# Two more head groups' queries and keys by seven block products, maxima 22 steps ahead, five partial head products early

## The chip, the cores and the metric

One core of a Trainium2 chip runs the kernel as one program. The time is the device time of the program on that core, in microseconds (us). Its engines work side by side, each through its own instructions in order: PE (TensorE) multiplies matrices into PSUM banks of 128 x 512 floats, ACT (ScalarE) and DVE (VectorE) read PSUM and SBUF, POOL (GpSimd) works on SBUF, and SP (SyncE) here issues all DMAs.

## The reference

Multi-head attention (32 heads of 16) and a gated feed-forward layer on the same input, mixed by a sigmoid of `x . gate_w`; all in float32, with S = 2048 tokens, D = 512, F = 1792.

```python
qkv = (x @ wqkv).reshape(B, S, 3, H, Dh).transpose(2, 0, 3, 1, 4)
p = softmax(einsum("bhqd,bhkd->bhqk", q, k) * Dh ** -0.5)
a = einsum("bhqk,bhkd->bhqd", p, v).transpose(0, 2, 1, 3).reshape(B, S, D) @ wo
b = (sigmoid(x @ w_gate) * (x @ w_up)) @ w_down
g = sigmoid((x * gate_w).sum(-1, keepdims=True))
return g * a + (1 - g) * b
```

## The kernel before

A float32 operand is split into a high part and a rest (`xh`, `xl`), and a product is three matmuls on the parts (`terms`). The program has four stages.

**Front and values.** Queries and keys of head group 0 (of four groups of eight heads) are computed (line 612), stored to DRAM (`q_d`, `k_d`) and loaded back for head pair 0 (`load_pair`, line 238). Then come the values of all heads (the loop at line 655), 192 slots of two half-height matmuls each. Between the slots, `first_max` issues the first score products for the row maxima: each call is two matmuls (line 284) and two DVE reductions (line 286). They start at slot 20.

**Steps.** The loop `for k in range(NPER)` has 256 steps; a head pair takes 16 of them. A step has eight score products for the exponentials (line 648, then ACT's `Exp`, line 650), the product of exponentials and values (line 781, 16 matmuls by the profile), eight score products for the maxima of a later pair (lines 284 and 286), and twelve half-height matmuls of "fill" (line 161). The maxima run LEAD = 20 half-steps ahead, so that they end at step FREE = 246. The last ten steps (order `LAST`) have no maxima and six fill matmuls. Row maxima of half a pair go through POOL (`put_max`) to DRAM and back as extra rows of the queries (line 308). `load_pair` of the next pair stands at a pair's first step.

**Fill** is a generator, `filling`, that hands out one product at a time: queries and keys of head groups 1 to 3 (`"qk"`, 24 matmuls a product), gate and up projections (`"far"`, `"side"`, `"chain"`) and the first half of the output product of EARLY = 3 blocks of 256 queries (`"heads"`). Gate and up are done with seven block products in place of eight (the weights' quarters and x's quarters are added and subtracted first, and the results added afterwards on POOL, lines 507 to 517). Weights are split on POOL. POOL's work is put into a list, `later` (additions, weights and splits in order of arrival), and `work(length)` issues some of it at two places of a step; `slow` holds the mixing of x. The two halves of a fill product write one PSUM bank: between the halves `turn` puts an empty instruction into POOL's order that waits for the first half, and the second half waits for it.

**Tail.** The hidden layer times `w_down` (line 966, 28 chunks of 24 matmuls), and for eight blocks u of 256 queries the product with `wo` (`heads_out`, line 940): 24 matmuls, or 12 where `u < EARLY`, which then add the first half from DRAM (`hp_d`).

PE, ACT, DVE and POOL run in the written order. The order of SP's DMAs is set by the scheduler that builds the program.

## Time and profile before

| | |
|---|---|
| median of 3 runs (lowest to highest) | 1694.38 us (1693.39 to 1695.08) |
| the profiled execution's own time | 1694.23 us |
| its span, first to last instruction | 1692.5 us |
| DMA over the span | 223.51 MB, mean 132 GB/s |
| granted clock of PE | 1.000 |

Rows of the profile name an engine, a line of the kernel, an operation, the tile written and the tiles read. A busy time counts overlapping instructions once; the mean of one instruction is its latency and can be longer than the distance to the next. In brackets stands the idle time before an instruction and what ended it.

### The profile page before, as it was taken

To read this page: it belongs to the slowest core of one execution; us is meant where nothing else is said; L and a number is where in the kernel's file an instruction comes from. 1 tells how busy PE (TensorE), PEld (TensorE's weight loads), DVE (VectorE), ACT (ScalarE), POOL (GpSimd) and SP (SyncE) were. 2 spreads that over 40 slices of the span, in tenths; PEclk is the share of its full clock that TensorE was granted. 3 is DMA by queue.
4 is the path that set the end of the run, shared out by engine and by line. 5 is a ranking of instruction groups with operands and counts; after the bars stand their busy time and mean duration, and the time that the engine had idled before them with its cause. 6 is when DMAs were issued, how large, how long until landed. Compare 5 with 4: busy or idle time off the path is not lost.

```text
span 1692.5 us, 34518 instructions
## 1 busy us (share of the span) xinstructions
PE 1685.8 (100%) x12509; PEld 1032.5 (61%) x12509; DVE 1446.7 (85%) x2333; ACT 1357.4 (80%) x2643; POOL 880.7 (52%) x862
## 2 busy tenths in 40 slices
PE   9999999999999999999999999999999999999999
PEld 7755555555555555555555555555555555568887
DVE  6988888888889989999888888889988888887643
ACT  4188888888898989888888989889898988984321
POOL 1033343447664555554666667676666667643110
PEclk9999999999999999999999999999999999999999
DMA  7412324254755352534625353535353434478762
GB/s 235 109 45 65 83 64 96 64 127 153 200 171 136 109 120 92 118 114 106 193 98 136 108 144 108 139 108 135 108 126 108 127 120 132 142 234 280 266 195 71
DMA packets 126922, 223.51 MB, mean 132 GB/s; under 512 B 23520, under 2 KB 33504, under 8 KB 123872
## 3 DMA queue, kind: packets, MB, share of 16 engines
q1 hardware_dynamic: 126752, 221.31, 44.9%
q8 instruction: 98, 1.61, 0.4%
q14 instruction: 72, 0.59, 0.1%
HBM read 131.33 MB, written 89.92 MB: 131 GB/s over the span
## 4 chain that ended last, share of the span: by engine, by line
PE 96%; DMA 1%; DVE 1%; POOL 1%; issue 0%; SPq 0%; ACT 0%; POOLq 0%; DVEq 0%
PE dn L161 30%; PE sm L781 27%; PE sm L284 12%; PE st L648 7%; PE sm L966 5%; PE sm L648 5%; PE st L284 2%; PE dn L966 2%; PE st L161 2%; PE st L966 2%; PE st L148 1%; PE st L612 1%; PE sm L148 1%; DVE stat L286 1%; DMA gul<-gu_d 1%
## 5 line engine op out<-in xcount | busy, mean ns | idle before, releaser
L286 DVE TENSOR_REDUCE stat<-sm 128x1 f32<-128x512 f32 x1310 | 848.5, 683 | 150.8 <-PE sm L648 129.6
L650 ACT ACTIVATE p<-st 128x512 f32<-128x512 f32 x1020 | 617.7, 652 | 1.4 <-PE st L648 0.8
L650 ACT ACTIVATE p<-sm 128x512 f32<-128x512 f32 x1026 | 608.8, 630 | 0.9 <-PE sm L648 0.9
L284 PE MATMUL sm<-ks,qs 48*128 48x512 f32 x1310 | 516.4, 435 | 0.3 <-DVE stat L286 0.3
L286 DVE TENSOR_REDUCE stat<-st 128x1 f32<-128x512 f32 x738 | 482.1, 681 | 0.1
L781 PE MATMUL sm<-p,v 128*17 128x512 f32 x4032 | 482.1, 595 | 0.0
L648 PE MATMUL sm<-qs,ks 64*128 64x512 f32 x1026 | 426.9, 419 | 0.3 <-DMA qs<-max_d 0.3
L648 PE MATMUL st<-qs,ks 64*128 64x512 f32 x1020 | 426.9, 419 | 0.2 <-DVE stat L286 0.2
L284 PEld LDWEIGHTS sm<-ks,qs 48*128 48x128 f32 x1310 | 233.9, 184 | 290.9 <-DVE stat L286 208.6
L798 POOL TENSOR_TENSOR sum<-sum,part 128x512 f32<-128x512 f32 x224 | 288.9, 1290 | 181.2 <-PE sm L648 169.1
L284 PE MATMUL st<-ks,qs 48*128 48x512 f32 x738 | 291.3, 395 | 0.0
L786 ACT ACTIVATE part<-sm 128x512 f32<-128x512 f32 x215 | 128.7, 599 | 133.0 <-issue 106.8
L781 PEld LDWEIGHTS sm<-p,v 128*17 128x17 f32 x4032 | 93.6, 96 | 227.2 <-issue 156.7
L648 PEld LDWEIGHTS st<-qs,ks 64*128 64x128 f32 x1020 | 187.7, 184 | 30.2 <-issue 3.4
L648 PEld LDWEIGHTS sm<-qs,ks 64*128 64x128 f32 x1026 | 189.1, 185 | 9.5 <-issue 4.3
L514 POOL TENSOR_TENSOR chain<-chain,chain 128x512 f32<-128x512 f32 x84 | 108.5, 1291 | 114.6 <-PE sm L648 112.1
L514 POOL TENSOR_TENSOR had<-chain,had 128x512 f32<-128x512 f32 x84 | 108.1, 1287 | 59.6 <-PE sm L648 43.0
L284 PEld LDWEIGHTS st<-ks,qs 48*128 48x128 f32 x738 | 137.8, 187 | 1.0 <-ACT v L631 0.3
L514 POOL TENSOR_TENSOR side<-side,side 128x512 f32<-128x512 f32 x28 | 36.1, 1291 | 92.7 <-PE sm L648 87.1
L576 ACT ACTIVATE chain<-dn 128x512 f32<-128x512 f32 x112 | 77.8, 694 | 0.0
L103 POOL TENSOR_TENSOR ol<-ot,oh 128x1024 fp32r<-128x1024 f32 (+1 forms) x8 | 16.4, 2054 | 101.9 <-ACT oh L100 101.9
L311 POOL CAST mhl<-mt 128x32 fp32r<-128x32 f32 x32 | 7.4, 233 | 102.7 <-DVE mt L292 102.7
(837 smaller groups left out, 3205.3 us busy)
## 6 DMA issues: line engine op xcount, KB each, us to landing
gul<-gu_d SPq DMA_DIRECT2D x56, 512.0 KB
had<-gu_d SPq DMA_DIRECT2D x84, 256.0 KB
gu_d<-had SPq DMA_DIRECT2D x84, 256.0 KB
gu_d<-side SPq DMA_DIRECT2D x56, 256.0 KB
qs<-q_d SPq DMA_DIRECT2D x90, 128.0 KB
ks<-k_d SPq DMA_DIRECT2D x90, 128.0 KB
pv_d<-sum SPq DMA_DIRECT2D x32, 256.0 KB
gu_d<-far SPq DMA_DIRECT2D x28, 256.0 KB
```

The lines of the kernel that those rows point to most:

```text
L148: pe.matmul(o, a, b, start=(i == 0), stop=(i == len(ops) - 1))
L161: mm = pe.matmul(self.o, a[rows], b[rows], start=(self.n == 0), stop=(self.n == 2 * len(self.ops) - 1))
L284: pe.matmul(t, qs[r:r + KM, qt * P:(qt + 1) * P], ks[r:r + KM, g * 512:(g + 1) * 512], start=True, stop=True)
L286: dve.tensor_reduce(stat[half][:, b, qt % 8, g:g + 1], t, axis=AX.X, op=ALU.max)
L514: pool.tensor_tensor(to, u, w, ALU.add)
L576: leave = lambda e, o: act.activation(e, o, AF.Copy)
L648: pe.matmul(o, ks[r:r + KR, (kt + a) * P:(kt + a + 1) * P], qs[r:r + KR, q0:q0 + 512], start=True, stop=True)
L650: act.activation(pt[:, 2 * a + c, :], o, AF.Exp, scale=DH ** -0.5)
L781: pe.matmul(o[32 * c:32 * c + VW, :], v[:, 2 * k % 16 + a, h * VW:(h + 1) * VW], pts[c // 2][:, 2 * a + c % 2, :], start=(a == 0), stop=(a ...
L786: act.activation(e, o, AF.Copy)
L798: pool.tensor_tensor(s, s, e, ALU.add)
L966: pe.matmul(down[t], a, b, start=(f == 0 and m == 0), stop=(f == NF - 2 and m == 5))
```

## The change

Queries and keys of head groups 2 and 3 are no longer jobs `"qk"` of the fill: their weights go through `"far"`, `"side"` and `"chain"`, with seven block products in place of eight; the results gather in a new DRAM tensor `s_d`. `kept_x` saves the two parts of x that are overwritten for this and needed again. Sixteen new pieces, `split_load` and `split_sum`, load `s_d` back in steps 75 to 122, split it on POOL and store it to `q_d` and `k_d`. POOL's work on weights goes to a list of their own, `turnover`, behind the additions in `later`. LEAD is 22, so that FREE is 245 and `first_max` has 44 calls, from slot 10. EARLY is 5; for the two new blocks eight more reciprocals on DVE are done early (steps 202 to 211). `load_pair` has two loads a head and operand in place of three: one of 32 rows and one of 16, with rows interleaved.

```diff
--- before.py
+++ after.py
...
 KR = 64
-LEAD = 20
+LEAD = 22
...
 FREE = NPER - LEAD // 2
-EARLY = 3
+EARLY = 5
...
     rec_d = dram.tile([P, 512], F32, name="rec_d")
-    t_d = dram.tile([3, 2, 2, 2, P, 512], F32, name="t_d")
+    t_d = dram.tile([5, 2, 2, 2, P, 512], F32, name="t_d")
+    s_d = dram.tile([2, 2, P, S], F32, name="s_d")
...
         else:
-            split_later(h, l, raw)
+            split_later(h, l, raw, queue=turnover)
...
-    later, slow, soon = [], [], []
+    later, turnover, slow, soon = [], [], [], []
     def work(length):
-        while length > 0.3 and (later or slow):
-            cost, step = (later or slow).pop(0)
+        while length > 0.3 and (later or turnover or slow):
+            cost, step = (later or turnover or slow).pop(0)
...
         return [(w[k], (xh[:, k, cols], xl[:, k, cols])) for k in range(KT)]
-
-    FORM = {0: (0, 1, 0), 1: (0, 0, 1)}
...
             for b in range(2):
-                rows = slice((2 * p + b) * DH, (2 * p + b + 1) * DH)
-                for i, a in enumerate(FORM[t]):
-                    r = 64 * b + i * DH
-                    sp.dma_start((QS, KS)[t][p % 2][r:r + DH, cols].bitcast(F32), src[a, rows, cols])
+                rows, r = slice((2 * p + b) * DH, (2 * p + b + 1) * DH), 64 * b
+                to = (QS, KS)[t][p % 2]
+                if t == 0:
+                    two, one = src[:, rows, cols].rearrange("a d s -> d a s"), src[0, rows, cols]
+                else:
+                    two, one = src[0, rows, cols].unsqueeze(1), src[1, rows, cols]
+                    two = two.to_broadcast([DH, 2, cols.stop - cols.start])
+                sp.dma_start(to[r:r + 2 * DH, cols].bitcast(F32), two)
+                sp.dma_start(to[r + 2 * DH:r + KM, cols].bitcast(F32), one)
...
+    def kept_x(n, c, k0, cx):
+        cols = slice(cx * 512, (cx + 1) * 512)
+        for a, xs in enumerate((xh, xl)):
+            sp.dma_start(t_d[n, a, c].rearrange("k p s -> p k s"), xs[:, k0:k0 + 2, cols].bitcast(F32))
+
...
         pairs = [(m, i) for i in range(HF) for m in range(2)]
-        jobs = ([("qk", n) for n in range(1, D // P)] + [("far", i) for i in range(HF)]
-                + [("side", n) for n in pairs] + [("chain", n) for n in pairs] + [("heads", 0), ("down", 0)])
+        qk = [(2, 0), (3, 0)]
+        jobs = [("qk", 1)] + [("far", i) for i in range(HF + 1)]
+        for ns in (qk, pairs):
+            jobs += [("side", n) for n in ns] + [("chain", n) for n in ns]
+        jobs += [("heads", 0), ("down", 0)]
         gu_w = (w_gate, w_up)
+
+        def beside(m, i):
+            return i + HF if m < 2 else i + 1
...
                     raw = keep.tile([P, KT, P], F32, name=f"far{m}{n}r", tag="wr", bufs=2)
-                    sp.dma_start(raw[:, 2:], gu_w[m][n][:, 2:])
+                    sp.dma_start(raw[:, 2:], gu_w[m][n][:, 2:] if n < HF else wqk[2, 1, :, m])
...
             m, i = n
+            if m >= 2:
+                return [raw_weights(wqk[f, :, :, m - 2].rearrange("b p k f -> p b k f"), [P, KT, P],
+                                    f"{kind}{m}_{f}") for f in (2, 3)]
...
                 ks = slice(*ks)
-                split_later(h[:, ks], l[:, ks], src[:, ks], cost=0.33 * (ks.stop - ks.start))
+                split_later(h[:, ks], l[:, ks], src[:, ks], cost=0.33 * (ks.stop - ks.start), queue=turnover)
...
             def op(to, u, w, how):
-                later.append((0.65, lambda: pool.tensor_tensor(to, u, w, how)))
+                turnover.append((0.65, lambda: pool.tensor_tensor(to, u, w, how)))
...
         def place(m, f, c):
-            return gu_d[m, f, :, c * 512:(c + 1) * 512]
+            to = gu_d[m, f] if m < 2 else s_d[m - 2, f]
+            return to[:, c * 512:(c + 1) * 512]
...
                         yield run
-                        sp.dma_start(place(m, n, c), out_of(run, f"far{m}{n}_{c}"))
+                        sp.dma_start(place(m, n, c) if n < HF else place(2 + m, 0, c), out_of(run, f"far{m}{n}_{c}"))
...
                         yield run
-                        if n == pairs[-1]:
+                        if n in (qk[-1], pairs[-1]):
...
                             first = e
-                            sp.dma_start(place(m, i + HF, c + 2), e)
+                            sp.dma_start(place(m, beside(m, i), c + 2), e)
...
                 for c in range(2):
-                    to = [place(m, i, c), place(m, i, c + 2), place(m, i + HF, c + 2), place(m, i + HF, c)]
+                    i2 = beside(m, i)
+                    to = [place(m, i, c), place(m, i, c + 2), place(m, i2, c + 2), place(m, i2, c)]
...
                         yield run
+                        if n == qk[-1] and a >= 2:
+                            mixed_x(1 + a, c, 2 * a - 4, c + 2)
...
-            ks, q0 = slice(2 * (u // 2), 2 * (u // 2) + 2), (u % 2) * 256
+            ks, q0 = slice(u // 2 % 2 * 2, u // 2 % 2 * 2 + 2), (u % 2) * 256
...
-        ask = {"qk": (0, 3), "far": (0, 1), "side": (0, 1), "chain": (1, 3), "heads": (0, 1)}
+        ask = {"qk": (0, 3), "far": (0, 1), "side": (0, 1), "chain": (0, 1), "heads": (0, 1)}
...
                     if at == 4:
-                        for u in range(EARLY):
+                        for u in range(4):
...
                         first_heads_split(at - 6)
-                if kind == "heads" and at == 2:
-                    first_heads_split(2)
+                if kind == "heads" and at in (2, 4, 6):
+                    if at == 2:
+                        first_heads_load(4)
+                    first_heads_split(at // 2 + 1)
...
                     new = weights(*nxt, coming)
-                    end = later[-1]
+                    end = turnover[-1]
                 yield run
-            while end in later:
-                later.pop(0)[1]()
+            while end in turnover:
+                turnover.pop(0)[1]()
             ws = new
-            if kind == "far" and n == HF - 1:
+            if kind == "far" and n == HF:
...
                     mixed_x(0, c, 2, c)
+                for c in range(2):
+                    kept_x(3, c, 0, c + 2)
+                    kept_x(4, c, 2, c + 2)
...
             for m in range(3 * KT):
-                if 12 * (t + g) + m >= 20 + (192 - 20) * (2 * LEAD - len(first)) // (2 * LEAD):
+                if 12 * (t + g) + m >= 10 + (192 - 10) * (2 * LEAD - len(first)) // (2 * LEAD):
...
                 two[1].half(1 - g)
-                if (0, 0) in mrow and g == UP and m == 2:
+                if (0, 0) in mrow and m == 2:
...
+    split_in = {}
+
+    def split_load(r):
+        f, t, c = r // 8, r // 4 % 2, r % 4
+        e = split_in[r] = keep.tile([P, 2, 512], F32R, name=f"sq{r}", tag="ev", bufs=2)
+        sp.dma_start(e[:, 0, :].bitcast(F32), s_d[t, f, :, c * 512:(c + 1) * 512])
+
+    def split_sum(r):
+        f, t, c = r // 8, r // 4 % 2, r % 4
+        e = split_in.pop(r)
+
+        def store():
+            for a in range(2):
+                sp.dma_start((q_d, k_d)[t][a, (2 + f) * P:(3 + f) * P, c * 512:(c + 1) * 512],
+                             e[:, 1 - a, :].bitcast(F32))
+        split_later(e[:, 1, :], e[:, 0, :], e[:, 0, :].bitcast(F32), store)
+
...
-    dens = [denominators(0, 0, 32, 8), denominators(0, 32, 64, 2), denominators(1, 0, 64, 2)]
+    dens = [chain(denominators(0, 0, 32, 8), denominators(1, 0, 32, 8)), denominators(0, 32, 64, 2),
+            denominators(1, 32, 64, 2)]
...
             leave = dve.tensor_copy
-        if 78 <= k < 126:
-            t, r = divmod(k - 78, 6)
-            if r == 0:
+        if 75 <= k < 123:
+            t, r = divmod(k - 75, 6)
+            if r in (0, 3):
+                split_load(2 * t + r // 3)
+            if r in (1, 4):
+                split_sum(2 * t + r // 3)
+            if r == 1:
...
             exps = iter([early[0]] * 4 + [early[1]] * 4)
-        if 192 <= k < 202:
+        if 192 <= k < 212:
...
             next(dens[1])

```

In the tail of PE's order, here is block u = 3 of the output product, behind its chunk of the hidden layer (`wohl` is `wo`, `oh` and `ol` the heads' parts). Before:

```order
L966 MATMUL sm_70<-wd1h,hl_18595 128x512
L148 MATMUL sm_69<-wohl,oh_18598 128x512 x2
L148 MATMUL sm_69<-wohl,ol_18599 128x512
L148 MATMUL sm_69<-wohl,oh_18598 128x512 x2
L148 MATMUL sm_69<-wohl,ol_18599 128x512
L148 MATMUL sm_69<-wohl,oh_18598 128x512 x2
L148 MATMUL sm_69<-wohl,ol_18599 128x512
L148 MATMUL sm_69<-wohl,oh_18598 128x512 x2
L148 MATMUL sm_69<-wohl,ol_18599 128x512
L148 MATMUL st_65<-wohl,oh_18598 128x512 x2
```

and of the change:

```order
L1015 MATMUL sm_70<-wd1h,hl_18752 128x512
L149 MATMUL sm_69<-wohl,oh_18755 128x512 x2
L149 MATMUL sm_69<-wohl,ol_18756 128x512
L149 MATMUL sm_69<-wohl,oh_18755 128x512 x2
L149 MATMUL sm_69<-wohl,ol_18756 128x512
L149 MATMUL st_65<-wohl,oh_18755 128x512 x2
```

Each of the block's two products has 6 matmuls in place of 12, and the same holds for block u = 4: 24 matmuls fewer.

In POOL's order, here is a chain job (`had` and `chain` rows are additions of results, `sum` rows additions of attention sums, `mhl` rows the maxima, `ca`, `cb` and `chain_..r` rows the next job's weights). Before:

```order
L514 TENSOR_TENSOR chain_01_12679<-chain_01_12679,chain_00_12609 128x512
L514 TENSOR_TENSOR had_00_12546<-chain_01_12679,had_00_12546 128x512
L798 TENSOR_TENSOR sum_1_12366<-sum_1_12366,part_12699 128x512
L426 TENSOR_TENSOR chain_3r<-chain_3r,chain_10r 128x256
L426 TENSOR_TENSOR chain_10r<-chain_10r 128x256
L426 TENSOR_TENSOR chain_10r<-chain_10r,chain_3r 128x256
L138 CAST ca(0, 3)h<-chain_3r 128x512
L135 TENSOR_TENSOR ca(0, 3)l<-chain_3r,ca(0, 3)h 128x512
L138 CAST cb(0, 3)h<-chain_10r 128x512
L135 TENSOR_TENSOR cb(0, 3)l<-chain_10r,cb(0, 3)h 128x512
L514 TENSOR_TENSOR chain_02_12752<-chain_02_12752,chain_01_12679 128x512
```

and of the change:

```order
L842 TENSOR_TENSOR sum_1_12550<-sum_1_12550,part_13015 128x512
L444 TENSOR_TENSOR chain_3r<-chain_3r,chain_10r 128x256
L444 TENSOR_TENSOR chain_10r<-chain_10r 128x256
L444 TENSOR_TENSOR chain_10r<-chain_10r,chain_3r 128x256
L139 CAST ca(1, 3)h<-chain_3r 128x512
L536 TENSOR_TENSOR had_00_13000<-chain_00_13076,had_00_13000 128x512
L136 TENSOR_TENSOR ca(1, 3)l<-chain_3r,ca(1, 3)h 128x512
L139 CAST cb(1, 3)h<-chain_10r 128x512
L136 TENSOR_TENSOR cb(1, 3)l<-chain_10r,cb(1, 3)h 128x512
L536 TENSOR_TENSOR chain_01_13147<-chain_01_13147,chain_00_13076 128x512
```

The weights, seven instructions in one piece before, now stand where no addition is left to do, and an addition that comes up goes between them.

In SP's order, here are the loads of pair 1's queries and keys (`qs`, `ks`) and what stands behind them, in the values' stage. Before:

```order
L107 DMA qk_0r<-in_wqk_dram 128x512
L107 DMA qk_1r<-in_wqk_dram 128x512
L244 DMA qs_101<-q_d 16x2048 x6
L244 DMA ks_102<-k_d 16x2048 x6
L304 DMA max_d<-mhl_0_859 128x64
L308 DMA qs_99<-max_d 1x32x32 x4
```

and of the change:

```order
L247 DMA qs_102<-q_d 32x1x2048
L248 DMA qs_102<-q_d 16x2048
L247 DMA ks_103<-k_d 32x1x2048
L248 DMA ks_103<-k_d 16x2048
L366 DMA t_d<-xh 128x2x512
L366 DMA t_d<-xl 128x2x512
L308 DMA max_d<-mhl_0_831 128x64
L403 DMA far00r<-in_w_gate_dram 128x256
L312 DMA qs_100<-max_d 1x32x32 x4
```

Eight loads stand where twelve stood (four of them are shown), and four stores of x (`t_d`, two of them shown) now stand ahead of the first maxima.

## The prediction, made before the run

> **What bounds the kernel now.** I read the busy shares, then the stages, and then the steps one by one.
>
> ```profile
> PE 1685.8 (100%) x12509; PEld 1032.5 (61%) x12509; DVE 1446.7 (85%) x2333; ACT 1357.4 (80%) x2643; POOL 880.7 (52%) x862
> ```
>
> PE is never without work; a gain has to take matmuls off it, or pauses that its busy time hides. The view by stages (front, values, steps with maxima, steps without, tail; columns: length, then busy us of PE, weight loads, DVE, ACT, POOL) shows who could take over:
>
> ```profile
> 27.25:84.66 57.41, 56.72 (x469) 43.83 (x469) 50.29 (x83) 10.48 (x19) 4.16 (x6) 1.00 0.49 129
> 84.66:1461.20 1376.54, 1376.05 (x10827) 796.30 (x10826) 1227.36 (x2071) 1223.35 (x2446) 810.41 (x811) 1.00 0.42 119
> 1461.20:1498.04 36.84, 36.49 (x273) 16.38 (x269) 28.83 (x41) 36.35 (x76) 15.29 (x15) 1.00 0.33 111
> 1498.04:1692.50 194.46, 190.35 (x845) 155.54 (x844) 121.43 (x109) 70.06 (x76) 42.48 (x20) 1.00 0.65 213
> ```
>
> In the steps DVE and ACT each have 11% left, in the last ten steps ACT is as full as PE (36.35 of 36.84), in the tail nobody but PE is near full. In the chain of waits, two neighbouring steps start their value products 5.58 us apart:
>
> ```profile
> 1084.44 1.84 PE sm L781 x16
> 1090.02 1.84 PE sm L781 x16
> ```
>
> The 246 steps at 5.58 would take 1372.7 of the stage's 1376.5 us: all pauses of all steps together are 3.8 us. PE's rows at the end of the maxima (value products, and one wait):
>
> ```profile
> 1447.56 1.91 PE L781 MATMUL sm<-p,v 128*17 128x512 f32 x16
> 1453.78 1.91 PE L781 MATMUL sm<-p,v 128*17 128x512 f32 x16
> ...
> 1459.35 1.91 PE L781 MATMUL sm<-p,v 128*17 128x512 f32 x16
> ...
> 1463.20 1.91 PE L781 MATMUL sm<-p,v 128*17 128x512 f32 x16
> ...
> 1466.79 0.47 PE L648 MATMUL sm<-qs,ks 64*128 64x512 f32 x1 [0.35 <-DMA qs<-max_d]
> ...
> 1467.87 1.91 PE L781 MATMUL sm<-p,v 128*17 128x512 f32 x16
> ...
> 1471.70 1.91 PE L781 MATMUL st<-p,v 128*17 128x512 f32 x16
> 1475.54 1.91 PE L781 MATMUL st<-p,v 128*17 128x512 f32 x16
> ```
>
> A step without maxima takes 3.84 us (1471.70 to 1475.54). One takes 4.67 (1463.20 to 1467.87), because PE waits for the last rows of maxima. The step from 1447.56 takes 6.22; that pause comes with the early hidden layer on DVE and stays.
>
> **The change part by part.**
>
> *The fill stays as long as it is.* Groups 2 and 3 cost 16 products of 24 half-height matmuls, 384. By blocks they cost 4 + 8 + 16 products of 12, 336. The two new head blocks add 4 products of 12, 48. The sum is 384 again, so the same 250 steps' worth of fill runs in the same twelve places a step, with six in each of the last steps; it then ends in step 254, one later than now, which nothing waits for. An ACT eviction comes with each product, so the steps of groups 2 and 3 get one a step, as all chain steps have, and those run at 5.58 already. The term is 0.
>
> *The tail loses 24 full-height matmuls.* Their price, 24 of this kind in a row in the chain of waits:
>
> ```profile
> 1628.81 5.44 PE st L148 x24
> ```
>
> That is **-5.44 us**. It counts in full only if PE sets the tail's end: 672 matmuls of the hidden layer and 156 of the heads at 5.44 / 24 = 0.227 us are 187.7 us, with the last value product (1.91) 189.6 of 194.46, and most of what is left comes after the last matmul. DVE gains four additions and loses half of two multiplications, against 73 us of slack. If PE did not set the end, the term would be 0; that is a rival.
>
> *A step is exchanged.* With LEAD 22 one step with maxima (5.58) becomes one without (3.84): **-1.74 us**. But ACT is full there. Its exponentials come every 0.48 us, eight a step, so 3.82 a step, and two exponentials of the early hidden layer now fall among them:
>
> ```profile
> 1460.59 0.81 ACT L724 ACTIVATE gul<-gul 128x256 f32<-128x256 f32 x2
> ...
> 1484.22 0.88 ACT L650 ACTIVATE p<-sm 128x512 f32<-128x512 f32 x1
> 1484.70 0.90 ACT L650 ACTIVATE p<-st 128x512 f32<-128x512 f32 x1
> ```
>
> The pair takes from 0 (hidden by the banks between PE and ACT) to 0.81. In the rows at 1484 ACT has no idle time ahead of either, so I take half, **+0.4**.
>
> *The wait for the last maxima.* The rows now have seven half-steps in place of five before they are used, one more step of 3.84 us, against a wait whose whole price is 4.67 - 3.84. I take all of it, **-0.83 us**; 0 if something else holds them.
>
> *The values' stage gets four more calls of maxima*, eight matmuls, two at a time. A pair takes 0.23:
>
> ```profile
> 33.28 0.39 PE L161 MATMUL dn<-wv_h,xl 64*128 64x512 f32 x1
> 33.51 0.40 PE L284 MATMUL sm<-ks,qs 48*128 48x512 f32 x2
> 33.74 0.40 PE L161 MATMUL st<-wv_h,xh 64*128 64x512 f32 x2
> ...
> 45.84 13.72 DVE L286 TENSOR_REDUCE stat<-sm 128x1 f32<-128x512 f32 x22 [0.42 <-PE sm L284]
> ...
> 23.23 2.73 SPq L244 DMA_DIRECT2D ks<-k_d  x6
> ```
>
> That is **+0.93 us**. DVE needs 13.72 / 11 = 1.25 us a call by the row of 22, with its waits in it; PE gives a call every 182 / 44 = 4.1 slots of 0.23 and one pair more, about 1.2. DVE is close to the bound: 44 calls at 1.25 are 55 us, and they must fit between slot 10 (about 29.6 us) and the end near 85.6. They fit with 1 us to spare. Slot 10 needs keys whose last load is issued by 26, and it is reached 2.7 us earlier than the first call today. So the term lies between 0.9 and 3.6; I take 0.93.
>
> *Nothing, with cover:* the loads of a pair. They are needed five steps after issue (27.9 us) in place of six (33.5):
>
> ```profile
> 528.56 2.64 SPq L244 DMA_DIRECT2D qs<-q_d x6
> 531.24 3.94 SPq L244 DMA_DIRECT2D ks<-k_d x6
> ...
> GB/s 131 131 123 123 131 119 150 340 289 18 10 0 113 150 207 244 307 29 0 0 16 0 0 43 219 129 238 307 160 207 156 115 33 0 4 21 8 207 318 0
> ```
>
> The last row has slices of 1 us from 535: the slow transfer ends at about 542, 13 us after the first issue. The cover is 15 us. POOL's work grows by 28 additions, while 16 splits of groups 2 and 3 take the place of 16 others:
>
> ```profile
> L514 POOL TENSOR_TENSOR chain<-chain,chain 128x512 f32<-128x512 f32 x84 | 108.5, 1291 | 114.6 <-PE sm L648 112.1
> ```
>
> That is 28 x 1.29 = 36 us, hidden by POOL's 48% idle time as long as no piece stands in front of the empty instruction that lets the second halves go; the additions, which release buffers, come first now, and weights are asked for earlier, so the bunches get smaller. Eight reciprocals on DVE fall into steps in which DVE waits 0.7 us a step for PE. I put these at 0, with the present 3.8 us of pauses as the scale: from half of them less (-1.9) to as much again (+3.8).
>
> The sum: -5.44 - 1.74 + 0.4 - 0.83 + 0.93 = **-6.7 us**. The profiled execution took 1694.23 (span 1692.5 and 1.7 around it), the median is 0.15 above it: 1687.5 by the one, 1687.7 by the other. I forecast **1687.6 us**.
>
> One rule speaks against the change. The profile has these pairs of equal instructions on DVE:
>
> ```profile
> 1449.14 1.53 DVE L728 TENSOR_SCALAR gul<-gul 128x512 f32<-128x512 f32 x1
> 1455.38 0.57 DVE L728 TENSOR_SCALAR gul<-gul 128x512 f32<-128x512 f32 x1
> ...
> 1498.34 1.52 DVE L739 CAST xh<-gul 128x512 fp32r<-128x512 f32 x1
> ...
> 1500.50 0.42 DVE L739 CAST xh<-gul 128x512 fp32r<-128x512 f32 x1
> ```
>
> The Trainium skill, page "Advanced Engine Details and Errata", section "VectorE Performance Modes", says that DVE's second SBUF port is shared with GpSimd, so that two-port DVE instructions and GpSimd's block each other. The slow ones of the pairs agree with it, at about 1 us each. By that rule more POOL work in the last steps (two more blocks to split) delays DVE there.
>
> **The rivals.**
>
> *POOL gets in DVE's way in the last steps* (chance 0.08). Each slow twin costs DVE 1.53 - 0.57 = 0.96 or 1.52 - 0.42 = 1.10 us; if two more of them stand ahead of a bank's eviction, PE waits about 2 us: 1689.6. Against it: DVE is busy 28.83 of 36.84 us there, so 8 us have to be used up first.
>
> *The tail does not give back* (0.06). If the loads of gate and up set the tail's pace, the 5.44 fall away: 1693.0. For it speaks DMA's share of 0.65 in the tail, against it PE's 190.35 of 194.46.
>
> *Slower: the new splits of groups 2 and 3 hold up PE* (0.13). `split_sum` waits on POOL for its load from `s_d`; the empty instruction for the next halves stands behind it, and PE's second half behind that. A load stands in SP's order behind stores that wait for POOL. POOL's waits have one such case, and PE one short pause in a step in which POOL was full:
>
> ```profile
> POOL sum L798 <- DMA mix<-in_xT_dram: 4.3, 1, 4.3
> PE st L648 <- DVE stat L286: 0.2, 1, 0.2
> ```
>
> Sixteen splits have to cost 6.7 / 16 = 0.42 us each to eat the gain, 0.63 each to be 3.4 us slower. If each cost 1 us, the time would be 1703.6; if the 4.3 came in full, more. Against it: with the 4.3 PE lost nothing to be seen, and the second half of a step is slack. I give 0.08 to a cost that ends near 1694 and 0.05 to more.
>
> *The pair loads come late* (0.03). If 32-row loads with interleaved rows ran at less than half the present speed (13 us becomes 30), 14 pairs would wait 2.1 us each: 1717. It decides from 27.9 us on.
>
> **How the numbers follow.** The forecast has 0.70, and its own range is 1685.3 (pauses halved, the pair of evictions hidden) to 1690.5 (ACT's 0.81 in full, 2.5 us in the values' stage or in pauses). About 0.2%, 3.4 us, is what a measurement tells from no change; faster is below 1691.0. Faster: the forecast but for 0.01, the port, and 0.02 of the rest, **0.79**. Same: the tail, 0.06 of the splits and a little of the others, **0.13**. Slower: **0.08**. The range that leaves out 2 in 10 is **1685.0 to 1692.0**: below it little is possible, since no more matmuls go, and above it lie the rivals but the port.
>
> **What would show it.** The tail from the first `w_down` matmul should be 189 us in place of 194.5; the values' stage 58.3; eleven steps at 3.84 to 3.9 with none at 4.67 and no wait for `max_d`; steps 16 to 71 at 5.58 as the others; no POOL wait for `s_d` above 4 us. It is wrong if the steps stage has more than 7 us of pauses above 5.58, or if PE waits in the tail.

## The result

| | before | changed |
|---|---|---|
| median (lowest to highest) | 1694.6 us (1693.39 to 1695.83), 12 runs | 1699.24 us (1696.12 to 1701.55), 12 runs |
| ratio to before | | 1.0025, 95% interval 1.0016 to 1.0034 |
| profiled execution, its span | 1694.23, 1692.5 us | 1699.21, 1697.4 us |
| DMA over the span | 223.51 MB | 254.20 MB |

The kernel became 0.25% slower, where 0.4% faster was forecast. Three of the 12 executions of the changed kernel have a mean granted clock of 1.000 and take 1696.12 to 1696.66 us, the other nine have 0.998 or 0.999 and take 1698.55 to 1701.55; the profile is of one of the nine. Of the changed kernel, the busy shares and the four stages of the prediction (same columns):

```profile
PE 1686.8 (99%) x12485; PEld 1030.4 (61%) x12485; DVE 1453.4 (86%) x2347; ACT 1365.5 (80%) x2657; POOL 938.1 (55%) x920
```

```profile
27.25:86.25 59.00, 58.32 (x479) 45.32 (x478) 54.74 (x91) 10.51 (x19) 4.22 (x6) 1.00 0.57 157
86.25:1466.28 1380.03, 1376.28 (x10783) 793.89 (x10782) 1225.99 (x2070) 1227.94 (x2450) 868.16 (x869) 1.00 0.46 139
1466.28:1507.09 40.81, 40.63 (x308) 18.64 (x305) 31.45 (x46) 40.81 (x86) 15.45 (x15) 1.00 0.24 75
1507.09:1697.40 190.31, 185.19 (x821) 151.02 (x820) 122.50 (x111) 69.07 (x76) 41.94 (x20) 1.00 0.68 224
```

Stages by themselves mislead here, since one step went from the second stage to the third. I cut at value products instead: the first one, and that of step 244, the 244 steps between them being steps with maxima in both kernels (steps are counted from the first value product, as 0). Before (its other two rows stand in the prediction: 1453.78 for step 244 and the tail's start at 1498.04) and changed:

```profile
88.90 1.91 PE L781 MATMUL sm<-p,v 128*17 128x512 f32 x16
```

```profile
90.48 1.91 PE L825 MATMUL sm<-p,v 128*17 128x512 f32 x16
...
1464.43 1.91 PE L825 MATMUL sm<-p,v 128*17 128x512 f32 x16
...
1507.09 0.50 PE L1015 MATMUL dn<-wd0h,xh 128*128 128x512 f32 x1
```

| piece | before | changed | difference | forecast |
|---|---|---|---|---|
| up to the first value product | 88.90 | 90.48 | +1.58 | +0.93 |
| 244 steps with maxima | 1364.88 | 1373.95 | **+9.07** | 0 |
| from there to the tail | 44.26 | 42.66 | -1.60 | -2.17 |
| tail | 194.46 | 190.31 | -4.15 | -5.44 |
| sum | | | +4.90 | -6.68 |

Three of four pieces came within 1.3 us of the forecast. Most of the 9.07 us are in few steps: the others take 5.58 or up to 0.26 more, but eight take 0.42 to 0.82 us more (20, 28, 36, 52, 84, 101, 108, 124; step 204 comes later in the text), and steps 56, 128 and 129 take 7.12, 9.05 and 6.33. The waits of PE's weight loads (engine, line, what is waited for: us in total, times, longest) name the cause's last link, before and changed:

```profile
PEld dn L161 <- POOLq L172: 2.6, 6, 0.6
```

```profile
PEld dn L162 <- POOLq L173: 9.7, 14, 2.6
```

POOLq is POOL's sequencer: PE waits for the empty instruction that `turn` puts between the halves of a fill product. Four of the waits, 2.2 us together, stand in the values' stage in both kernels; so the steps have two before (0.45 us) and ten in the changed kernel (7.55 us). What stands ahead of the empty instruction on POOL differs. Step 28 of the changed kernel, from the timelines of DVE, POOL and PE's weight loads:

```profile
249.59 0.21 DVE L296 STREAM_TRANSPOSE mt<-mpad 128x32 f32<-128x32 f32 x1
...
249.86 0.21 POOL L315 CAST mhl<-mt 128x32 fp32r<-128x32 f32 x1 [2.14 <-DVE mt L296]
250.15 0.26 POOL L306 TENSOR_TENSOR mhl<-mt,mhl 128x32 fp32r<-128x32 f32 x1
250.35 0.40 POOL L139 CAST far04h<-far04r 128x256 fp32r<-128x256 f32 x1
250.83 0.74 POOL L136 TENSOR_TENSOR far04l<-far04r,far04h 128x256 fp32r<-128x256 f32 x1
251.52 0.39 POOL L139 CAST far14h<-far14r 128x256 fp32r<-128x256 f32 x1
...
252.02 0.18 PEld L162 LDWEIGHTS dn<-xh,far03h 64*128 64x128 f32 x1 [0.45 <-POOLq L173]
```

A half pair's maxima end in this step. POOL's first instruction for them (`mhl`) stands at the head of its queue and waits 2.14 us for DVE's transpose; three pieces of the next job's weights follow, and only then (251.91) the empty instruction, 0.45 us too late for PE. In the kernel before, the same two bunches lie one step apart (POOL):

```profile
380.17 0.40 POOL L138 CAST far02h<-far02r 128x256 fp32r<-128x256 f32 x1
...
381.79 0.73 POOL L135 TENSOR_TENSOR far12l<-far12r,far12h 128x256 fp32r<-128x256 f32 x1
...
387.24 0.21 POOL L311 CAST mhl<-mt 128x32 fp32r<-128x32 f32 x1 [0.96 <-DVE mt L292]
```

LEAD 22 puts the end of a half pair's maxima one step earlier, onto the step in which far and side jobs split their weights. In steps 84 and 108 the two bunches meet as well, but there the waits for the empty instruction (0.23 us each) come one step later, in 85 and 109, and PE's weight loads wait for DVE, which does a product for the gate logits (line 812) right behind the transpose:

```profile
567.14 0.18 PEld L288 LDWEIGHTS sm<-ks,qs 48*128 48x128 f32 x1 [0.37 <-DVE stat L290]
```

Step 128, the first chain job of gate and up, is another case (SP's issues, POOL, PE):

```profile
807.63 0.51 SPq L108 DMA_DIRECT2D chain_0r<-in_w_up_dram  x1
808.19 0.44 SPq L108 DMA_DIRECT2D chain_7r<-in_w_up_dram  x1
...
817.11 0.72 POOL L444 TENSOR_TENSOR chain_0r<-chain_0r,chain_7r 128x256 f32<-128x256 f32 x1 [3.80 <-DMA chain_7r<-in_w_up_dram]
817.91 0.72 POOL L444 TENSOR_TENSOR chain_7r<-chain_7r 128x256 f32<-128x256 f32 x1
...
818.75 0.49 PE L162 MATMUL dn<-xh,cb(0, 0)h 64*128 64x512 f32 x1 [2.19 <-POOLq L173]
...
821.15 2.66 PE L825 MATMUL sm<-p,v 128*17 128x512 f32 x16
```

POOL comes to the next job's weights 5.1 us after the second load was issued (817.11 - 3.80 - 808.19); the load takes 8.9. Again the empty instruction stands behind, and PE does nothing for 2.19 us. The value product after it takes 2.66 in place of 1.91 us, of which more at the end.

### The profile page after: what moved, and what is told of

Same layout as the page of the kernel before. It is cut to its first block, busy times and chain, and to the rows that moved or that the text cites. A ratio compares the mean times of both kernels' runs of the same rounds, so it can differ in the third digit from the quotient of the medians.

```text
span 1697.4 us, 34663 instructions
## 1 busy us (share of the span) xinstructions
PE 1686.8 (99%) x12485; PEld 1030.4 (61%) x12485; DVE 1453.4 (86%) x2347; ACT 1365.5 (80%) x2657; POOL 938.1 (55%) x920
## 2 busy tenths in 40 slices
DMA packets 143756, 254.20 MB, mean 150 GB/s; under 512 B 24224, under 2 KB 36512, under 8 KB 140704
## 4 chain that ended last, share of the span: by engine, by line
PE 97%; DMA 1%; POOL 1%; issue 1%; DVE 0%; ACT 0%; SPq 0%; POOLq 0%; DVEq 0%
PE dn L162 29%; PE sm L825 27%; PE sm L288 12%; PE st L675 7%; PE sm L1015 5%; PE sm L675 5%; PE st L288 3%; PE st L162 2%; PE dn L1015 2%; PE st L1015 2%; PE st L639 1%; PE st L149 1%; PE sm L149 1%; DMA chain_7r<-in_w_up_dram 1%; DMA chain_3r<-in_wqk_dram 0%
## 5 line engine op out<-in xcount | busy, mean ns | idle before, releaser
L536 POOL TENSOR_TENSOR chain<-chain,chain 128x512 f32<-128x512 f32 x96 | 124.1, 1292 | 166.8 <-PE sm L675 148.6
L536 POOL TENSOR_TENSOR had<-chain,had 128x512 f32<-128x512 f32 x96 | 123.5, 1287 | 29.8 <-PE sm L675 14.8
L603 ACT ACTIVATE chain<-dn 128x512 f32<-128x512 f32 x128 | 88.7, 693 | 0.0
L536 POOL TENSOR_TENSOR side<-side,side 128x512 f32<-128x512 f32 x32 | 41.3, 1292 | 84.8 <-PE sm L675 69.8
L104 POOL TENSOR_TENSOR ol<-ot,oh 128x512 fp32r<-128x512 f32 (+1 forms) x8 | 14.5, 1810 | 98.4 <-ACT oh L101 98.4
```

Source lines behind the costliest of these rows:

```text
L536: pool.tensor_tensor(to, u, w, ALU.add)
L603: leave = lambda e, o: act.activation(e, o, AF.Copy)
```

## The experiments

Theory A (steps 56, 128 and 129): POOL stands at weights whose load has not landed (the change asks for them one product earlier in chain jobs, and works on them two products earlier). Theory B (the eight steps): the meeting of maxima and weights on POOL. Rival C: the extra traffic or the extra instructions, spread over the steps. Every diff is against the changed kernel unless it says otherwise; the runs of the kernel before beside them had medians of 1693.93, 1694.05 and 1694.18 us in the three groups. "244 steps" is measured as in the table above (before 1364.88, changed 1373.95).

### Chain jobs ask for their weights as before

```diff
-"chain": (0, 1), "heads"
+"chain": (1, 3), "heads"
```

> The change with one entry put back: in chain jobs the next weights are loaded from the job's second product on and worked on from its fourth on, as before the change, in place of first and second. Theory A (POOL stands at weights whose load has not landed, the empty instruction stands behind them, and PE's second half behind that): steps 56, 128 and 129 lose their 1.54 + 3.47 + 0.75 = 5.8 us of excess over 5.58, the time falls from 1699.2 to about 1693.5. Theory B (the excess comes from maxima that POOL waits for on DVE, ahead of weights): only steps 20 to 52 and 84 to 124 matter, so within 1 us of 1699. Theory C (more DMA bytes slow everything): 1699.

1693.41 us, ratio to before 0.9994 (0.9985 to 1.0003). 244 steps: 1368.68, 5.3 less than the change. Steps 56, 128 and 129 are at 5.58; the pauses of B are all there, and one of 0.78 comes in step 130, because the load is now issued ten us later too (817.91 in place of 808.19). A holds, at its price.

### The maxima's POOL instructions half a step later

```diff
-        for half in list(mrow):
-            later[:0] = put_max(half)
         work(2.6)
+        for half in list(mrow):
+            later[:0] = put_max(half)
```

> The change with POOL's two instructions for a finished half pair's maxima queued one half-step later, behind the work at a step's end and not ahead of it. Theory B (POOL waits there up to 2 us for DVE's transpose, the weights of the fill queue behind it and the empty instruction behind them): the pauses of 0.42 to 0.82 us in steps 20, 28, 36, 52, 84, 101, 108 and 124 go, 4.0 us in all, 1699.2 becomes about 1695.2; step 128 stays at 9 us. Theory A alone: under 0.5 us. Theory C: nothing.

**1689.17 us, ratio 0.9968 (0.9956 to 0.9981)**: 10.1 us less than the change, not 4.0. 244 steps: 1363.81. The pauses of B are gone, as expected, but for 0.3 us in each of steps 84 and 108, where DVE's part stays. Steps 56 and 128 are at 5.58 as well, which was not expected. POOL and SP show how (POOL in the step that was 28 before; SP and POOL ahead of step 128):

```profile
248.16 0.41 POOL L139 CAST far14h<-far14r 128x256 fp32r<-128x256 f32 x1
...
250.81 0.21 POOL L315 CAST mhl<-mt 128x32 fp32r<-128x32 f32 x1 [0.17 <-PE sm L675]
```

```profile
790.90 0.33 SPq L108 DMA_DIRECT2D chain_0r<-in_w_up_dram  x1
792.83 0.33 SPq L108 DMA_DIRECT2D chain_7r<-in_w_up_dram  x1
...
807.14 0.75 POOL L444 TENSOR_TENSOR chain_0r<-chain_0r,chain_7r 128x256 f32<-128x256 f32 x1
```

The weights go first and POOL's 2.14 us of waiting for `mt` are gone. And SP issues the chain loads two steps earlier, the first of them 9.8 us ahead of step 127 (which starts at 800.69) in place of 1.1 us behind its start (806.51 in the change): moving two POOL instructions made the scheduler put these loads ahead of the last reloads of x, and POOL reaches the weights 14 us after their issue, without a wait.

### Both edits

```diff
-"chain": (0, 1), "heads"
+"chain": (1, 3), "heads"
...
-        for half in list(mrow):
-            later[:0] = put_max(half)
         work(2.6)
+        for half in list(mrow):
+            later[:0] = put_max(half)
```

> Both edits of the two kernels ahead of it. If A and B each hold and add up: 5.8 + 4.0 = 9.8 us less than the change, 1689.4, and the steps with maxima have at most 3 us above 5.58 in all, as before the change. Theory C: the pauses stay, 1699.

1689.06 us, ratio 0.9966 (0.9954 to 0.9979). 244 steps: 1363.90. The expected time, though not as a sum of 5.8 and 4.0: the second edit alone has it all, since it removes A's wait in its own way. C is out: with all bytes and all additions of the change the steps are 1.0 us shorter than before it.

### POOL's work in one list

```diff
-    later, turnover, slow, soon = [], [], [], []
+    later, slow, soon = [], [], []
+    turnover = later
```

> The change with POOL's work in one list again (weights in order of arrival among the additions, not behind them). If the order of the list makes the pauses: they go, about 1690. If it is where POOL waits (A and B), the list matters little: the additions that stood ahead of the weights now stand behind them, POOL's wait for the load of step 128 comes a little earlier or later, 1697 to 1701.

1697.95 us, ratio 1.0022 (1.0013 to 1.0032). 244 steps: 1371.01. Step 56 loses 1.0 us, step 128 0.6 us, step 129 its whole 0.75 us, the pauses of B stay. PE's pause in step 128 is no shorter than in the change (2.40 us), but its clock stays at 1.00 after it, of which more at the end. The order within the list, on which the prediction relied, matters little either way.

### LEAD 20 in the changed kernel

```diff
-LEAD = 22
+LEAD = 20
-                if 12 * (t + g) + m >= 10 + (192 - 10) * (2 * LEAD - len(first)) // (2 * LEAD):
+                if 12 * (t + g) + m >= 20 + (192 - 20) * (2 * LEAD - len(first)) // (2 * LEAD):
-                if (0, 0) in mrow and m == 2:
+                if (0, 0) in mrow and g == UP and m == 2:
```

> The change with LEAD 20 and first maxima from slot 20 again; everything else of the change stays. If the pauses of steps 20 to 52 and 84 to 124 come from the step in which a half pair's maxima end (LEAD 22 puts it where the fill's weights are split, LEAD 20 one step later), they go: 4.0 us less in the steps, 1.6 less in the values' stage, 1.7 + 0.3 more in the last steps. With the pauses of steps 56 and 128 unchanged that is 1699.2 - 3.6 = 1695.6; if these depend on the same instructions through the order of SP's loads, they go too: about 1690. If the pauses come from the new additions or the bytes, they stay: about 1699.5.

1698.97 us, ratio 1.0025 (1.0015 to 1.0034): near the third time, but not for its reason. The pauses of steps 20 to 52 are gone, as B has it, and steps 56 and 128 are at 5.58, but the 244 steps take 1373.11, because another wait appears. PE's waits of this kernel:

```profile
PE st L675 <- DMA qs<-max_d: 3.5, 3, 2.7
```

Step 54 takes 10.01 us: 2.67 of the 4.43 above 5.58 are this wait, and most of the rest is PE's clock, which was granted at 0.50 to 0.51 from 398 to 401. The way of its rows of maxima on SP's queue, the score product that needs them, and a wait of SP's queue between 380 and 400:

```profile
388.11 0.33 SPq L308 DMA_DIRECT2D max_d<-mhl  x1
...
394.67 2.86 SPq L312 DMA_DIRECT2D qs<-max_d  x4
...
397.57 0.76 PE L675 MATMUL st<-qs,ks 64*128 64x512 f32 x1 [2.67 <-DMA qs<-max_d]
```

```profile
SPq L312 <- DMA max_d<-mhl: 4.2, 1, 4.2
```

The reload waits until the store has landed, 6.6 us after the store's issue; in the kernel before, the rows stored at 387.81 were reloaded at 390.11. Why this store is slower is not shown; DMA moved 136 to 412 GB/s in the eight us from 386 here, and 0 to 262 in the five us from 386 before. With LEAD 20 the rows have two half-steps less, and in this step that is no longer enough, though it was before the change. So the change without LEAD 22 runs into another wait, and LEAD 22 brings the meeting on POOL. In steps 77 and 101 pauses of 1.3 and 1.2 us remain, with waits of 0.62 for the empty instruction; I did not follow them further. The first value product starts at 88.60 here, 1.9 us earlier than with LEAD 22.

### The kernel before, with the maxima's instructions later

Against the kernel before:

```diff
-        for half in list(mrow):
-            later[:0] = put_max(half)
         work(2.6)
+        for half in list(mrow):
+            later[:0] = put_max(half)
```

> The kernel before with the two POOL instructions of the maxima queued one half-step later. A control: if this order helps only where weights stand behind the maxima, which LEAD 20 avoids, nothing changes: 1693.9, within 1 us. If the order is worth something by itself, whatever the change, 2 us or more are gained here too.

1720.89 us, ratio 1.0153 (1.014 to 1.0167): 27 us slower, where nothing was expected. PE's waits:

```profile
PE st L648 <- DMA qs<-max_d: 16.8, 19, 2.3
```

24 of the 30 steps in which a half pair's maxima end, counted to step 238, now take 6.0 to 8.2 us (238: 7.87). At LEAD 20 the rows of maxima have no half-step to give; at LEAD 22 the same edit costs nothing. The control shows that the edit is no gain by itself, and what LEAD 22 buys: room for this delay.

### EARLY 3

With the maxima's instructions later, and:

```diff
-EARLY = 5
+EARLY = 3
...
-                        for u in range(4):
+                        for u in range(EARLY):
                             first_heads_load(u)
...
-                if kind == "heads" and at in (2, 4, 6):
-                    if at == 2:
-                        first_heads_load(4)
-                    first_heads_split(at // 2 + 1)
+                if kind == "heads" and at == 2:
+                    first_heads_split(2)
```

> The change with the maxima's POOL instructions later (1689.2) and EARLY 3 in place of 5: the tail has its 24 matmuls again. If they count in full, the tail is 5.44 us longer and the wait of 1.3 us for the late weights of w_down remains: 1694.6. If that wait is there only because the two further blocks' work delays ACT or the loads, it goes and the price is 4.1: 1693.3. If the tail is set by loads, no change: 1689.2.

1693.79 us, ratio 0.9996 (0.9987 to 1.0005), 4.62 above the same kernel with EARLY 5. Tail from the first `w_down` matmul to the end of the span: 1692.1 - 1497.33 = 194.77, against 1687.4 - 1496.96 = 190.44. Nearly the second reading: PE's wait for `wd5l` in it is 0.4 us, against 1.3 with EARLY 5. With the maxima later, the whole gain over the kernel before comes from these 24 matmuls.

### Twelve loads a pair

With the maxima's instructions later, and:

```diff
-                to = (QS, KS)[t][p % 2]
...
-                sp.dma_start(to[r:r + 2 * DH, cols].bitcast(F32), two)
-                sp.dma_start(to[r + 2 * DH:r + KM, cols].bitcast(F32), one)
+                for i, a in enumerate(((0, 1, 0), (0, 0, 1))[t]):
+                    sp.dma_start((QS, KS)[t][p % 2][r + i * DH:r + i * DH + DH, cols].bitcast(F32), src[a, rows, cols])
```

> The change with the maxima's POOL instructions later (1689.2) and the pair loads as twelve of 16 rows again. If the form of the loads is hidden, 1689.2 within 1 us. If eight loads are what keeps SP's queue short in the steps in which a pair begins, the weights' load of step 128 comes later again and a pause of 1 to 4 us shows there: 1690 to 1693.

1688.87 us, ratio 0.9967 (0.9954 to 0.9979). The form of the loads is hidden. One pause of 0.5 us comes back in step 56, none in 128.

### Weights one step later, maxima where the change has them

```diff
-        ask = {"qk": (0, 3), "far": (0, 1), "side": (0, 1), "chain": (0, 1), "heads": (0, 1)}
+        ask = {"qk": (0, 3), "far": (0, 2), "side": (0, 2), "chain": (1, 3), "heads": (0, 1)}
```

> The change with the maxima's POOL instructions left where they are, and the weights moved instead: chain jobs ask as before the change (1693.4 by that alone), far and side jobs work on the next weights from their third product on in place of the second, one step later. If the pauses come from the meeting of the two (POOL waits for DVE's maxima, weights behind, empty instruction behind these), moving this partner does the same as moving the other: the pauses of steps 20 to 52 and 84 to 124 go, 4 us, 1689.4. If they come from POOL's wait for the maxima alone, they stay: 1693.4. If weights one step later come too late for their job, new pauses of 1 to 2 us at the ends of far and side jobs: above 1695.

1691.2 us (1688.99 to 1694.13), ratio 0.9977 (0.9969 to 0.9986), 1.8 us above the 1689.4 that the meeting was to give. The profile is of its longest execution. In it the pauses of B are gone (28, 36, 52, 101 and 124 at 5.58; 84 and 108 keep 0.3, as they do in the second experiment; 20 keeps 0.57), and 3 us lie in step 130, where POOL waits for a chain load, as in theory A. For the steps of B, moving the other partner does the same as moving the maxima: it is the meeting.

### ACT's late weights ahead of the sigmoid

With both edits, and in the tail:

```diff
-    act.activation(g1, logit, AF.Sigmoid)
-    hidden(2)
-    dve.tensor_scalar(g0, g1, -1.0, 1.0, op0=ALU.mult, op1=ALU.add)
...
     late_next()
+    act.activation(g1, logit, AF.Sigmoid)
+    hidden(2)
+    dve.tensor_scalar(g0, g1, -1.0, 1.0, op0=ALU.mult, op1=ALU.add)
     at = dict(
```

> The kernel with both edits (1689.1), and in the tail ACT's first splits of the late w_down weights ahead of the sigmoid of the gate logits and not behind it: about 2.3 us earlier on ACT and so for the loads that wait for their buffers. If the tail's 0.7 to 1.3 us wait of PE for wd5 comes from these loads' late start, it goes: tail 189.0 to 189.2, 1687.8 to 1688.4. If it comes from traffic of the other loads at that time, it stays: 1689.1.

1691.71 us, ratio 0.998 (0.9971 to 0.9988): 2.7 us slower by the medians than without it. The wait grew, from 0.67 us in the kernel with both edits to 1.14 + 0.86. PE and ACT of this kernel:

```profile
1512.35 0.49 PE L1014 MATMUL dn<-wd5h,hl 128*128 128x512 f32 x1 [1.14 <-ACT wd5h L101]
1513.70 0.56 PE L1014 MATMUL dn<-wd5l,hl 128*128 128x512 f32 x1 [0.86 <-POOL wd5l L104]
```

```profile
1511.67 0.63 ACT L101 ACTIVATE wd5h<-late 128x512 fp32r<-128x512 f32 x1 [4.87 <-DMA pv_d<-sum]
```

`wd5h` takes the buffer of the last attention sum, and waits until that sum is stored. The store was issued at 1505.94 and waited for until 1511.67, 5.7 us. The first reading is out: with ACT's splits earlier the wait did not go. For the second, traffic, speaks the order on SP's queue: the load of late weights that the edit brought forward now holds up two loads of gate and up, so that these go out from 1502.64, 3.3 us ahead of the store; with both edits all four loads of gate and up go out from 1497.29 to 1499.41, over 6 us ahead of it. That they slow the store is likely, but not shown. The wait is also not the whole price: behind it the granted clock is 0.50, 0.50, 0.50 and 0.79 in the four us from 1514, 1.7 us lost, where the kernel with both edits has 1.00.

### Chain weights one product later, loads unchanged

```diff
-"chain": (0, 1), "heads"
+"chain": (0, 2), "heads"
```

> The change with one number altered: in chain jobs the weights' loads are asked for at the first product as in the change, and POOL works on them from the third product on in place of the second. If POOL only has to reach the weights after the load has landed (it waited 3.8 us for it in step 128, a step is 5.58): the pauses of steps 56, 128 and 129 go, 1693.4. If the load slips back by as much, because SP's order follows POOL's, part of them stays: 1695 to 1698.

1693.18 us, ratio 0.9992 (0.9983 to 1.0001). 244 steps: 1368.12. SP and POOL:

```profile
806.61 0.46 SPq L108 DMA_DIRECT2D chain_7r<-in_w_up_dram  x1
```

```profile
815.75 0.75 POOL L444 TENSOR_TENSOR chain_0r<-chain_0r,chain_7r 128x256 f32<-128x256 f32 x1
```

The load stands where the change has it, POOL comes 9.1 us after its issue in place of 5.1 and finds it landed. The pauses of steps 56, 128 and 129 are gone, those of B untouched. A is settled: it is the distance between load and use on POOL.

The kernel with the maxima's instructions half a step later, alone or with the chain entry put back, beats both the kernel before (0.9968 and 0.9966) and the change.

## Why the prediction was wrong, step by step

**Fill, 0.** Right: steps without a meeting take 5.58 as before.

**Tail, -5.44.** The 24 matmuls went, but a wait ate most of what is missing: the stage is 4.15 shorter. Of the changed kernel, ACT, SP and PE in the tail, and ACT and SP of the kernel before:

```profile
1516.27 0.33 SPq L844 DMA_DIRECT2D pv_d<-sum  x1
...
1520.72 0.63 ACT L101 ACTIVATE wd5h<-late 128x512 fp32r<-128x512 f32 x1 [5.57 <-DMA pv_d<-sum]
...
1521.40 0.50 PE L1015 MATMUL dn<-wd5h,hl 128*128 128x512 f32 x1 [0.37 <-ACT wd5h L101]
1522.76 0.50 PE L1015 MATMUL dn<-wd5l,hl 128*128 128x512 f32 x1 [0.85 <-POOL wd5l L104]
```

```profile
1507.24 0.33 SPq L800 DMA_DIRECT2D pv_d<-sum  x1
...
1510.41 0.63 ACT L100 ACTIVATE wd5h<-late 128x512 fp32r<-128x512 f32 x1 [4.66 <-DMA pv_d<-sum]
```

From the store's issue to its landing pass 4.45 us in place of 3.17, and PE waits 1.22 us in place of 0.26, which is 0.96 of the missing 1.29. Why the store takes longer is not shown. That some of the tail would not come back was a rival, with the loads of gate and up as its cause; the place here is one store.

**Step exchange, ACT's two exponentials, wait for the last maxima: -1.74 + 0.4 - 0.83 = -2.17.** Measured -1.60. No wait for `max_d` is left and no step of 4.67, but one of 4.34, from 1468.27, at the end of which PE waits for an exponential:

```profile
1468.27 1.91 PE L825 MATMUL sm<-p,v 128*17 128x512 f32 x16
1472.11 0.50 PE L675 MATMUL st<-qs,ks 64*128 64x512 f32 x1 [0.18 <-ACT p L677]
1472.61 2.02 PE L825 MATMUL sm<-p,v 128*17 128x512 f32 x16
1476.54 2.01 PE L825 MATMUL st<-p,v 128*17 128x512 f32 x16
```

The next steps take 3.90 to 3.94. ACT is busy in all 40.81 us of the stage. If the other two terms are as forecast, the exponentials cost -1.60 + 1.74 + 0.83 = 0.97, above the upper bound of 0.81 and not half of it: 0.50 in the step from 1468.27, and about 0.1 in each of several steps behind it.

**Values' stage, +0.93.** Measured +1.58, between the bounds (0.9 to 3.6); against LEAD 20 in the changed kernel 1.9. The sum of LEAD 22's own terms is then near 0 (+1.58 - 1.60).

**Pair loads, 0.** Right, by the run with twelve.

**Reciprocals, 0.** All but one: step 204, in which a half pair's maxima end, takes 6.04 us, and 6.04 to 6.06 in every run of the change with LEAD 22. With LEAD 20 it is step 205 (6.06), where they then end.

**POOL's work, 0: the step that failed.** The prediction put it so: "hidden by POOL's 48% idle time as long as no piece stands in front of the empty instruction that lets the second halves go; the additions, which release buffers, come first now, and weights are asked for earlier, so the bunches get smaller". The condition was the right one. It was not looked up for the two things that could break it: which steps LEAD 22 moves `put_max` to, and how long after its issue a load is first used on POOL. Asking earlier made no bunch smaller; it moved POOL's use from 12.9 us behind the second load (before, issued 827.60, used 840.54) to 5.1. Against bounds of -1.9 and +3.8 the term was +9.07; with one line moved it is 1363.81 - 1364.88 = -1.07, within them. By the rows, the +9.07 are about 4.2 us of waits behind A's loads, 3.4 of waits at B's meetings, 0.6 on DVE (what stays in steps 84 and 108 with the maxima moved), 1.6 of slower clock behind A's longest wait, and smaller parts either way; the clock had no term in the prediction. Both signs by which the prediction was to be wrong came: the 244 steps have 1373.95 - 244 x 5.58 = 12.4 us of pauses, and PE waits in the tail.

**Rivals.** The slower one had the mechanism, the empty instruction behind a POOL instruction that waits, and named the wrong instruction. In three of the fourteen waits (0.23, 0.49 and 0.23 us, steps 85, 101 and 109) a `split_sum` is part of the bunch on POOL, but none waited for its load there, and with the maxima moved and every split in place these waits are gone. The port rival decided nothing: DVE has one slow twin in the last steps (`xl<-gul,xh`, 1.80 at 1487.60 against 0.69 at 1484.24), while POOL adds attention sums (1487.57, 1.28 us). The Trainium skill's rule, "Advanced Engine Details and Errata", section "VectorE Performance Modes", agrees with that row. The step it falls in takes 4.10 against 3.93, but that this is the price is not shown: the kernel before has such a twin too (1.78 at 1478.67), in a step of 3.83, and the run with EARLY 3 has one (1.66 at 1477.88) in a step of 3.92.

**The forecast time** of 1687.6 is close to what the change does without the two meetings, 1689.1 to 1689.2, but that is in part luck: with the maxima's instructions later, the values' stage, the last steps and the tail come 0.72, 0.51 and 1.42 us above their terms, and the 244 steps 1.07 below theirs.

## What to carry to other kernels

An engine's idle share says nothing about a hand-written order: where another engine waits for a mark in it, ask for every instruction ahead of the mark what it waits for itself, and put the one that waits last. When two periodic pieces of work share such an engine, a change of a lead or a count shifts their phase; go through the period for meetings. A load asked for earlier is no gain if its use moves forward by more.

## What the runs showed of the hardware

Idle PE can cost more than the idle time. The stretches after the pause of step 128 (length; busy us of PE, weight loads, DVE, ACT, POOL; then granted clock, DMA share, GB/s):

```profile
819.00:820.00 1.00, 1.00 (x8) 0.84 (x8) 0.00 (x0) 0.41 (x1) 1.00 (x3) 0.65 1.32 213
820.00:821.00 1.00, 1.00 (x5) 0.42 (x3) 0.99 (x2) 0.81 (x3) 1.00 (x2) 0.50 0.82 170
821.00:822.00 1.00, 1.00 (x8) 0.17 (x11) 0.30 (x1) 0.95 (x2) 1.00 (x2) 0.50 0.97 195
822.00:824.00 2.00, 2.00 (x18) 0.53 (x12) 0.00 (x0) 0.07 (x1) 1.92 (x3) 0.82 0.85 301
```

After 2.19 us without a matmul the granted clock goes to one half shortly after PE resumes (818.75). By these rows the stretch at one half lasts about 3.4 us and loses 0.35 + 0.50 + 0.50 + 0.36 = 1.7 us; steps 128 and 129 lose 1.6 us beyond the wait of 2.63 us that the weight loads had (3.47 + 0.75 = 4.2). In step 130 of the run with far and side weights one step later, a pause of 1.34 us did the same (clock 0.50 from 824 to 827). The length of the pause alone does not decide it. In step 56 PE had no matmul for 1.09 us (1.53 on the weight loads), and the clock stayed at 1.00. It also stayed there behind longer pauses: 2.32 us in step 118 of the kernel before with the maxima's instructions later, and 2.40 us in step 128 of the run with POOL's work in one list, the same place as above:

```profile
817.52 0.50 PE L162 MATMUL dn<-xh,cb(0, 0)h 64*128 64x512 f32 x1 [2.40 <-POOLq L173]
```

```profile
819.00:820.00 1.00, 1.00 (x13) 0.29 (x16) 0.84 (x2) 1.00 (x3) 1.00 (x1) 1.00 0.92 268
```

What decides it beside the length is not shown. The Trainium skill, page "TensorE: Matmul & The Clock Gate", section "Part 1: The HAM clock gate", gives half rate after an idle window of about 3.4 us and as long again to come back. The length of the slow stretch agrees; the pauses that brought it here were shorter than the page's window, and longer ones than these did not always bring it.

SP's chain loads moved by two steps (11 us against the steps) when two POOL instructions were moved by half a step. Where a scheduler places the DMAs, a pause can go or come by an edit that does not touch it.
